# Ten extra products of zeros on TensorE around the first rows of the first batch

## The chip, the cores and the metric

The kernel runs on one core of a Trainium2 chip. The metric is the device time of one execution in microseconds (us). The engines are named as in the profile: PE is TensorE (the matrix engine; PEld is its loading of weights), DVE is VectorE, ACT is ScalarE, POOL is GpSimd and SP is SyncE, whose queue issues nearly all loads here.

## The reference

The kernel computes channel attention and then a gated convolution. B = 4 batches, N = 6336 rows, C = 256 channels; the weights of the second part are 256 by 256 and the convolution has 5 taps.

```python
qn = q / (norm(q, axis=1) + 1e-6)          # norms over the N rows
kn = k / (norm(k, axis=1) + 1e-6)
s  = kn.T @ qn / tau                       # per batch: 256 x 256 scores
a  = softmax(s, axis=-1)
x  = v @ a                                 # N x 256
gate = sigmoid(causal_conv5(x, conv_w))    # per channel
out  = (gate * (x @ w_val)) @ w_out
```

## The kernel before

**Scores of a batch.** The 6336 rows of q and k are laid over 128 partitions, 49 rows on each and a rest of 64 rows. They are loaded in 17 groups (one row and the rest, then 16 groups of three rows) into six buffers named `raw`. For each row PE adds a product of the row's k and q to a bank of PSUM, `s_ps`, which holds the 256 x 256 scores; there is one such bank, so a batch can't start before the last batch's scores were copied out (ACT, L242, tile `s`). A product of zeros (`clear`, L231) opens the bank, and all later products add to it. Most rows of batch 0 go through PE as plain float32 (L226, `s_ps<-raw`; the trace holds two records for each such product). Some rows, one of the three in each of groups 11 to 16 of batch 0 and all rows of later batches, go in three products of split numbers instead: ACT rounds the row (L192, tile `hi`), POOL forms what is left (L193), and PE multiplies the parts (`s_ps<-hi`).

**Norms.** ACT squares each group (L209, into one of two buffers `sq`), and DVE and POOL add the squared rows up (L214, `acc_ps` on DVE and `acc` on POOL). In batch 0 DVE adds two rows a group up to group 10 and three from group 11 on. When all are added, DVE joins the two sums (L240, `acc_all`), and PE sums over the partitions (L245, L247). From there the softmax runs through ACT and DVE, and PE transposes its result (L285) before the first products of the second part.

**Weights.** DVE prepares the two weight matrices, which come as 64-bit floats, in some nine steps each (L132 to L154, tiles `w_raw`, `wa`, `wb`). These steps stand between the additions of batch 0. They need `moe_conv_w` to have landed.

**Second part.** For each of 13 chunks of 508 rows a batch, PE transposes v (L335, `t_ps`), ACT and DVE split it (L336 `v_hi`, L337 `v_lo`), PE forms x (L345, `x_ps`), DVE applies the five taps (L361), and PE forms the value product (`val_ps`) and the output product (L404, `o_ps`). Scores of the next batch run between these.

**Order.** The code issues the steps in a written order, but the framework's scheduler then orders each engine's instructions by a time model of its own. An edit of one place can so move instructions elsewhere. PE, DVE, ACT and POOL each run their list in the order given. Lines behind the edit are numbered 9 higher in the changed kernel (L231 is L236 there, L240 is L249, L245 is L254, L361 is L370).

Of the kernel before, what the change touches and what calls it, by code (L numbers as in the profile page):

```python
# [17 lines left out]
P = 128  # L18
# [10 lines left out]
def kernel(  # L29
# [13 lines left out]
    nc = tc.nc  # L43
# [43 lines left out]
    zeros = const.tile([P, 2 * C], F32R, name="zeros")  # L87
# [78 lines left out]
    def score_group(b, g):  # L166


        n = groups[g][1]
        raw = raws.pop((b, g))  # L170
        if b == 0:
            nw, nv = (GROUP, 2) if g < SIDE else (2, 3)
        else:
            nw, nv = (GROUP, 1 if g else 2) if b == 1 and g < LEAD else (0, 2)
        parts = [(P, 0, n)]
        if g == 0 and REST:
            parts.append((REST, n, 1))
        if g == 0:
            state[b] = dict(
                s=ps_s.tile([P, NH, C], F32, name="s_ps"),  # L180
                acc=ps_s.tile([P, 2, C], F32, name="acc_ps"),
                side=acc_p.tile([P, 2, C], F32, name="acc"),
                begun=set(),
            )
        st = state[b]
        split = [(np_, max(j0, nw), j0 + nj) for np_, j0, nj in parts if j0 + nj > nw]
        hi = split_p.tile([P, GROUP, 2, 2, C], F32R, name="hi") if split else None
        sq = split_p.tile([P, GROUP, 2, C], F32, name="sq", bufs=2)
        cast = None
        for np_, ja, jb in split:  # L190
            r, js = slice(0, np_), slice(ja, jb)
            cast = nc.scalar.copy(hi[r, js, :, 0, :], raw[r, js, :, :])  # L192
            nc.gpsimd.tensor_tensor(hi[r, js, :, 1, :], raw[r, js, :, :], hi[r, js, :, 0, :].bitcast(F32), ALU.subtract)  # L193
        rows = [(np_, j) for np_, j0, nj in parts for j in range(j0, j0 + nj)]
        where = {}
        with tc.issue_after(cast.ins) if cast else nullcontext():
            squares = [(np_, j0, j0 + nj) for np_, j0, nj in parts]
            for key in ("acc", "side"):
                if key not in st["begun"]:

                    full = [j for np_, j in rows if np_ == P and (j < nv) == (key == "acc")]
                    if full:
                        st["begun"].add(key)
                        where[full[0]] = key
                        nc.scalar.activation(st[key], raw[:, full[0]], AF.Square)
                        squares = [(np_, x, y) for np_, ja, jb in squares
                                   for x, y in ((ja, min(jb, full[0])), (max(ja, full[0] + 1), jb)) if x < y]
            for np_, ja, jb in squares:
                nc.scalar.activation(sq[0:np_, ja:jb], raw[0:np_, ja:jb], AF.Square)  # L209
        for np_, j in rows:  # L210
            if j in where:
                continue
            eng, key = (nc.vector, "acc") if j < nv else (nc.gpsimd, "side")
            eng.tensor_tensor(st[key][0:np_], st[key][0:np_], sq[0:np_, j], ALU.add)  # L214

        def mms(np_, j):
            r = slice(0, np_)
            stop = g == NG - 1 and np_ == parts[-1][0] and j == parts[-1][1] + parts[-1][2] - 1
            for h in range(NH):
                hs = slice(h * P, (h + 1) * P)  # L220
                if j < nw:
                    ops = [(raw[r, j, 1, hs], raw[r, j, 0, :])]
                else:
                    ops = [(hi[r, j, 1, x, hs], hi[r, j, 0, y, :]) for x, y in ((0, 0), (0, 1), (1, 0))]
                for n_, (lhs, rhs) in enumerate(ops):
                    nc.tensor.matmul(st["s"][:, h, :], lhs, rhs, start=False,  # L226
                                     stop=stop and h == NH - 1 and n_ == len(ops) - 1)

        def clear():

            nc.tensor.matmul(st["s"].rearrange("p h c -> p (h c)"), zeros[:, 0:P], zeros, start=True, stop=False)  # L231

        return ([clear] if g == 0 else []) + [lambda np_=np_, j=j: mms(np_, j) for np_, j0, nj in parts for j in range(j0, j0 + nj)]


    def softmax(b):  # L236
# [209 lines left out]
    def split_group():  # L446
        nonlocal issued
        if issued < len(all_groups):
            b, g = all_groups[issued]
            issued += 1  # L450
            load_upto(issued + PREFETCH)
            ready.append((b, g, score_group(b, g)))
# [154 lines left out]
```

## Time and profile before

| what | us |
|---|---|
| three runs | 657.83, 655.65, 657.69 |
| median of the three | 657.69 |
| the profiled execution | 655.7 |
| its span, first to last instruction | 653.8 |

The rows below come from the profiled execution, whose time is 1.9 us above its span and 2.0 us below the median of the three runs. A timeline row gives a start, a length, and how often the same instruction follows itself (xN); in brackets stands the engine's idle time before it and what ended it. A product's length contains its way through the array, so starts, not lengths, tell the pace of products in a row.

### The profile page before, as it was taken

Reading aid. Unit: us, or ns where it says so; the run is one execution under the profiler, and the core shown is the slowest. Engines: PE = TensorE matmul, PEld = TensorE weight load, DVE = VectorE, ACT = ScalarE, POOL = GpSimd, SP = SyncE. Lnnn points to the kernel's source line nnn. Section 1 sums busy time; section 2 is a strip of 40 time slices with the busy share of each in tenths; the row PEclk is TensorE's granted clock in tenths of the full one; section 3 lists DMA queues with packets and bytes.
Section 4 is the critical chain, followed back from the end, with each engine's and each line's share of the span. In section 5 each row is a group of like instructions: output and inputs, shape, how many; then the busy total and the mean of one; then the engine's idle time right before and its main releaser. Section 6 shows DMA issues by size and latency. Waiting matters only on the chain.

```text
span 653.8 us, 10657 instructions
## 1 busy us (share of the span) xinstructions
PE 636.1 (97%) x4008; PEld 570.3 (87%) x4008; DVE 521.7 (80%) x831; ACT 465.7 (71%) x607; POOL 362.1 (55%) x174
## 2 busy tenths in 40 slices
PE   7999999999999999999998999999999999999996
PEld 5878799998979999999997998999999798988886
DVE  3897689787878688778788688778778889888894
ACT  5465978867888768668688787777777755655564
POOL 2441896965837769659565497766763122312221
PEclk9999999999999999999999999999999999999999
DMA  8999875555635665545554375653222343443213
GB/s 272 336 320 335 267 233 154 152 170 162 188 99 175 186 195 176 167 136 173 177 178 127 113 222 168 179 182 103 65 80 76 113 126 102 114 129 105 65 51 99
DMA packets 107875, 105.75 MB, mean 162 GB/s; under 512 B 5744, under 2 KB 107312, under 8 KB 107824
## 3 DMA queue, kind: packets, MB, share of 16 engines
q1 hardware_dynamic: 82048, 79.76, 39.8%
q10 hardware_dynamic: 25776, 25.32, 13.7%
q8 instruction: 31, 0.51, 0.3%
q14 instruction: 20, 0.16, 0.1%
HBM read 79.11 MB, written 25.95 MB: 161 GB/s over the span
## 4 chain that ended last, share of the span: by engine, by line
PE 84%; DVE 4%; ACT 4%; DMA 3%; SPq 2%; POOL 1%; issue 1%; ACTq 0%; DVEq 0%
PE o_ps L404 21%; PE x_ps L345 19%; PE val_ps L345 19%; PE s_ps L226 17%; PE t_ps L335 6%; SPq L74 2%; DMA raw<-in_k_dram 1%; PE o_ps L294 1%; POOL hi L193 1%; DMA w_raw<-in_moe_conv_w_dram 1%; DMA v_raw<-in_v_dram 1%; ACT hi L192 1%; DVE acc_ps L214 1%; DVE gate L361 1%; DVE gate L374 1%
## 5 line engine op out<-in xcount | busy, mean ns | idle before, releaser
L361 DVE SCALAR_TENSOR_TENSOR gate<-x_ps,wa,gate 128x508 f32<-128x508 f32 (+1 forms) x416 | 275.4, 718 | 14.4 <-ACT gate L359 13.4
L193 POOL TENSOR_TENSOR hi<-raw,hi 128x1536 fp32r<-128x1536 f32 (+2 forms) x54 | 167.8, 3109 | 92.8 <-ACT hi L192 92.8
L388 POOL TENSOR_TENSOR g_lo<-gate,g_hi 128x1016 fp32r<-128x1016 f32 (+1 forms) x50 | 116.8, 2335 | 145.1 <-ACT g_hi L387 130.5
L214 DVE TENSOR_TENSOR acc_ps<-acc_ps,sq 128x512 f32<-128x512 f32 (+1 forms) x134 | 93.5, 698 | 73.9 <-ACT sq L209 70.7
L345 PE MATMUL x_ps<-v_hi,w 128*128 128x512 f32 (+1 forms) x416 | 138.1, 391 | 0.0
L345 PE MATMUL val_ps<-v_hi,w 128*128 128x508 f32 (+1 forms) x416 | 133.9, 384 | 0.8 <-ACT o_sb L414 0.7
L226 PE MATMUL s_ps<-hi 128*128 128x256 f32 (+1 forms) x852 | 121.0, 287 | 6.2 <-ACT hi L192 4.0
L226 PEld LDWEIGHTS s_ps<-hi 128*128 128x128 f32 (+1 forms) x852 | 110.7, 190 | 12.6 <-ACT hi L192 5.5
L404 PE MATMUL o_ps<-wo_hi,g_hi 128*128 128x256 f32 x400 | 113.3, 283 | 0.2 <-DVE gate L374 0.2
L414 ACT COPY o_sb<-o_ps 128x512 f32<-128x512 f32 x99 | 58.1, 588 | 76.1 <-PE o_ps L404 74.8
L404 PE MATMUL o_ps<-wo_lo,g_hi 128*128 128x256 f32 x400 | 112.2, 281 | 0.0
L404 PE MATMUL o_ps<-wo_hi,g_lo 128*128 128x256 f32 x400 | 111.8, 280 | 0.0
L209 ACT ACTIVATE sq<-raw 128x1536 f32<-128x1536 f32 (+3 forms) x69 | 96.0, 1393 | 16.3 <-DVE acc_ps L214 8.0
L214 POOL TENSOR_TENSOR acc<-acc,sq 128x512 f32<-128x512 f32 x58 | 76.3, 1315 | 38.9 <-ACT sq L209 38.5
L345 PEld LDWEIGHTS val_ps<-v_hi,w 128*128 128x128 f32 x416 | 77.2, 188 | 14.4 <-ACT o_sb L414 0.9
L345 PEld LDWEIGHTS x_ps<-v_hi,w 128*128 128x128 f32 x416 | 77.5, 188 | 13.9 <-DVE gate L361 0.2
L359 ACT ACTIVATE gate<-x_ps,wa 128x508 f32<-128x508 f32 (+1 forms) x104 | 68.1, 669 | 20.6 <-PE x_ps L345 20.3
L336 ACT CAST v_hi<-t_ps 128x512 fp32r<-128x512 f32 (+1 forms) x104 | 55.7, 568 | 35.7 <-PE t_ps L335 33.2
L345 PE MATMUL x_ps<-v_lo,w 128*128 128x512 f32 (+1 forms) x208 | 79.8, 384 | 0.0
L345 PE MATMUL val_ps<-v_lo,w 128*128 128x508 f32 (+1 forms) x208 | 79.3, 381 | 0.0
L374 DVE TENSOR_TENSOR gate<-val_ps,gate 128x508 f32<-128x508 f32 (+1 forms) x104 | 64.3, 657 | 17.1 <-ACT gate L367 14.4
L404 PEld LDWEIGHTS o_ps<-wo_hi,g_hi 128*128 128x128 f32 x400 | 75.3, 188 | 1.4 <-DVE gate L374 0.4
(84 smaller groups left out, 800.0 us busy)
## 6 DMA issues: line engine op xcount, KB each, us to landing
raw<-in_q_dram SPq DMA_DIRECT2D x64, 384.0 KB
raw<-in_k_dram SPq DMA_DIRECT2D x64, 384.0 KB
v_raw<-in_v_dram SPq DMA_DIRECT2D x44, 512.0 KB
out_dram<-o_sb ACTq DMA_DIRECT2D x47, 384.0 KB
out_dram<-o_sb ACTq DMA_DIRECT2D x47, 124.0 KB
v_raw<-in_v_dram SPq DMA_DIRECT2D x4, 384.0 KB
raw<-in_q_dram SPq DMA_DIRECT2D x4, 128.0 KB
raw<-in_k_dram SPq DMA_DIRECT2D x4, 128.0 KB
```

Source lines behind the costliest of these rows:

```text
L193: nc.gpsimd.tensor_tensor(hi[r, js, :, 1, :], raw[r, js, :, :], hi[r, js, :, 0, :].bitcast(F32), ALU.subtract)
L209: nc.scalar.activation(sq[0:np_, ja:jb], raw[0:np_, ja:jb], AF.Square)
L214: eng.tensor_tensor(st[key][0:np_], st[key][0:np_], sq[0:np_, j], ALU.add)
L226: nc.tensor.matmul(st["s"][:, h, :], lhs, rhs, start=False, stop=stop and h == NH - 1 and n_ == len(ops) - 1)
L336: nc.scalar.copy(th[:, h, 0:w], tp[:, 0:w])
L345: marks["PRODUCT"] = nc.tensor.matmul(ps, wt[:, which, ws, ch, hs], vs[:, ch, lo:hi_], start=n_ == 0, stop=n_ == 3 * NH - 1)
L359: nc.scalar.activation(gate[:, h, 0:w], x_ps[:, 0:w], AF.Copy, scale=cw[:, h, 0:1])
L361: nc.vector.scalar_tensor_tensor(gate[:, h, 0:w], x_ps[:, tap:tap + w], cw[:, h, tap:tap + 1], gate[:, h, 0:w], ALU.mult, ALU.add)
L374: nc.vector.tensor_tensor(gate[:, h, 0:w], val_ps[:, 0:w], gate[:, h, 0:w], ALU.mult)
L388: nc.gpsimd.tensor_tensor(gl[:, :, 0:w], gate[:, :, 0:w], gh[:, :, 0:w].bitcast(F32), ALU.subtract)
L404: nc.tensor.matmul(o_ps[:, u * C:(u + 1) * C], gs[:, h, off:off + P], ws[:, h, :], start=n_ == 0, stop=n_ == 3 * NH - 1)
L414: marks["ACT"] = nc.scalar.copy(o_sb[:, j:j + len(pair), :], o_ps[:, 0:len(pair) * C].rearrange("p (j c) -> p j c", c=C))
```

## The change

The function that makes the list of products of a group gets a helper, `idle(n)`, which issues n products of zeros with zeros into the score bank of the batch. They add zero. For group 0 of batch 0 alone, six of them stand behind `clear`, two behind the first row's product, and two behind the rest's product, which makes ten. Each is a 128x512 product.

```diff
+        def idle(n):
+
+            for _ in range(n):
+                nc.tensor.matmul(st["s"].rearrange("p h c -> p (h c)"), zeros[:, 0:P], zeros, start=False, stop=False)
+
         def clear():
 
-            nc.tensor.matmul(st["s"].rearrange("p h c -> p (h c)"), zeros[:, 0:P], zeros, start=True, stop=False)
-
-        return ([clear] if g == 0 else []) + [lambda np_=np_, j=j: mms(np_, j) for np_, j0, nj in parts for j in range(j0, j0 + nj)]
+            return nc.tensor.matmul(st["s"].rearrange("p h c -> p (h c)"), zeros[:, 0:P], zeros, start=True, stop=False)
+
+        products = [lambda np_=np_, j=j: mms(np_, j) for np_, j0, nj in parts for j in range(j0, j0 + nj)]
+        if (b, g) == (0, 0):
+
+            return [clear, lambda: idle(6)] + [f for p in products for f in (p, lambda: idle(2))]
+        return ([clear] if g == 0 else []) + products
```

The scheduler's order changes with it, far beyond these products. On PE, where batch 0's scores end and batch 1's begin, the list before is this (`acc_all` is the sum of squares, `t_ps` the transposed v, `a` the softmax's result):

```order
L226 MATMUL s_ps<-hi 128x256 x6
L231 MATMUL s_ps<-zeros 128x512
L226 MATMUL s_ps<-raw 128x256 x4
L245 MATMUL o_ps<-acc_all,ones 128x256
L247 MATMUL o_ps<-ones,acc_all 128x1 x2
L226 MATMUL s_ps<-raw 128x256 x6
L335 MATMUL t_ps<-ident,v_raw 128x128 x8
L226 MATMUL s_ps<-raw 128x256 x18
L285 MATMUL o_ps<-ident,a 128x128 x4
```

And this is the same place on PE in the changed kernel:

```order
L226 MATMUL s_ps<-hi 128x256 x6
L254 MATMUL o_ps<-acc_all,ones 128x256
L256 MATMUL o_ps<-ones,acc_all 128x1 x2
L344 MATMUL t_ps<-ident,v_raw 128x128 x8
L236 MATMUL s_ps<-zeros 128x512
L226 MATMUL s_ps<-raw 128x256 x28
L294 MATMUL o_ps<-ident,a 128x128 x4
```

The products on `acc_all` and the transposes of v now stand ahead of batch 1's opening product and its first rows. The same 28 row products stand ahead of the transposes of `a` in both.

On DVE, where the weight steps begin between the additions of batch 0, the difference is this (- is before, + is the change):

```order
 L214 TENSOR_TENSOR acc_ps<-acc_ps,sq 64x512
-L214 TENSOR_TENSOR acc_ps<-acc_ps,sq 128x512 x11
+L214 TENSOR_TENSOR acc_ps<-acc_ps,sq 128x512 x10
 L132 TENSOR_SCALAR wa<-w_raw 128x522
-L214 TENSOR_TENSOR acc_ps<-acc_ps,sq 128x512
 L134 SCALAR_TENSOR_TENSOR w_raw<-w_raw,wa 128x522
+L214 TENSOR_TENSOR acc_ps<-acc_ps,sq 128x512
 L136 TENSOR_SCALAR wa<-w_raw 128x522
+L132 TENSOR_SCALAR wb<-w_raw 128x512
+L214 TENSOR_TENSOR acc_ps<-acc_ps,sq 128x512
```

One addition fewer stands ahead of the first weight step, and the steps of the second matrix (`wb`) begin earlier. Further on, where the weight steps end, the difference is this:

```order
+L154 TENSOR_TENSOR wa<-wa,w_raw 128x522
 L146 TENSOR_TENSOR w_raw<-w_raw,wb 128x512
-L214 TENSOR_TENSOR acc_ps<-acc_ps,sq 128x512 x13
+L214 TENSOR_TENSOR acc_ps<-acc_ps,sq 128x512 x16
 L161 RECIPROCAL rtau<-tau_sb 128x1
 L214 TENSOR_TENSOR acc_ps<-acc_ps,sq 128x512 x6
-L240 TENSOR_TENSOR acc_all<-acc_ps,acc 128x512
+L249 TENSOR_TENSOR acc_all<-acc_ps,acc 128x512
```

Three additions more are left behind the last weight step.

A third place is the first chunks of the second part, about 75 to 85 us into the span. On DVE there, before, with `w` the product weights and `gate` the taps' sum:

```order
L299 TENSOR_TENSOR w<-o_ps,w 128x512
L361 SCALAR_TENSOR_TENSOR gate<-x_ps,wa,gate 128x508 x3
L214 TENSOR_TENSOR acc_ps<-acc_ps,sq 128x512 x2
L337 TENSOR_TENSOR v_lo<-t_ps,v_hi 128x512 x2
L214 TENSOR_TENSOR acc_ps<-acc_ps,sq 128x512 x2
L374 TENSOR_TENSOR gate<-val_ps,gate 128x508 x2
```

And in the changed kernel:

```order
L308 TENSOR_TENSOR w<-o_ps,w 128x512
L370 SCALAR_TENSOR_TENSOR gate<-x_ps,wa,gate 128x508 x2
L214 TENSOR_TENSOR acc_ps<-acc_ps,sq 128x512
L370 SCALAR_TENSOR_TENSOR gate<-x_ps,wa,gate 128x508
L214 TENSOR_TENSOR acc_ps<-acc_ps,sq 128x512 x3
L346 TENSOR_TENSOR v_lo<-t_ps,v_hi 128x512 x2
L383 TENSOR_TENSOR gate<-val_ps,gate 128x508 x2
```

Two additions that stood behind the splitting of v (`v_lo`) now stand ahead of it. On ACT the square that they add (L209) moves with them, from behind the two casts of v (L336, `v_hi`) to ahead of them.

Beyond these places, PE's list also differs in how output products, x products and score products interleave, from here to about 190 us and again from about 360 to 450 us; between the two stretches it is the same. SP loads `moe_w_val` and tau one group of q and k earlier, and `moe_w_out` one group earlier.

## Rows read from the trace of the kernel before

**Rows 1.** First line of the page.
```profile
span 653.8 us, 10657 instructions
```

**Rows 2.** Windows of the span: us, busy us of each engine (instructions), PEclk, DMA share, GB/s.
```profile
85.00:350.00 265.00, 264.21 (x1744) 239.91 (x1743) 215.72 (x342) 205.31 (x259) 184.39 (x82) 1.00 0.56 169
...
360.00:648.00 288.00, 286.54 (x1860) 259.18 (x1858) 235.84 (x380) 195.66 (x274) 133.60 (x60) 1.00 0.40 116
```

**Rows 3.** Windows of PE's first microseconds, same columns.
```profile
4.20:8.20 4.00, 3.95 (x8) 2.34 (x8) 0.69 (x1) 1.76 (x3) 0.00 (x0) 1.00 1.00 305
...
12.20:13.80 1.60, 1.60 (x5) 1.30 (x4) 1.26 (x2) 1.00 (x1) 1.18 (x1) 1.00 1.09 348
13.80:16.00 2.20, 2.20 (x11) 1.90 (x11) 1.40 (x2) 1.42 (x2) 1.27 (x1) 1.00 1.10 349
```

**Rows 4.** PE by line and form, 8.2 to 13.3 us, then 14 to 38.
```profile
L226 PE MATMUL s_ps<-raw 128*128 128x256 f32 x12 | 5.5, 648 | 0.0
...
L226 PE MATMUL s_ps<-raw 128*128 128x256 f32 x113 | 24.7, 381 | 0.0
```

**Rows 5.** PE's timeline, 0 to 95 us: start, us, what, idle before.
```profile
1.60 0.80 PE L231 MATMUL s_ps<-zeros 128*128 128x512 f32 x1 [1.60 <-DVE zeros L88]
4.25 34.65 PE L226 MATMUL s_ps<-raw 128*128 128x256 f32 x136 [1.85 <-DMA raw<-in_k_dram]
...
39.22 0.86 PE L226 MATMUL s_ps<-hi 128*128 128x256 f32 x5 [0.21 <-POOL hi L193]
...
43.54 0.86 PE L226 MATMUL s_ps<-hi 128*128 128x256 f32 x5 [0.98 <-POOL hi L193]
...
54.83 0.50 PE L231 MATMUL s_ps<-zeros 128*128 128x512 f32 x1 [0.67 <-DMA v_raw<-in_v_dram]
55.16 2.08 PE L226 MATMUL s_ps<-raw 128*128 128x256 f32 x8
57.18 0.70 PE L245 MATMUL o_ps<-acc_all,ones 128*128 128x256 f32 x2
...
69.39 0.60 PE L285 MATMUL o_ps<-ident,a 128*128 128x128 f32 x4
```

**Rows 6.** DVE's timeline, 20 to 58 us.
```profile
21.07 0.70 DVE L214 TENSOR_TENSOR acc_ps<-acc_ps,sq 128x512 f32<-128x512 f32 x1 [0.81 <-ACT sq L209]
22.08 0.66 DVE L132 TENSOR_SCALAR wa<-w_raw 128x522 int32<-128x522 int32 x1 [0.31 <-DMA w_raw<-in_moe_conv_w_dram]
...
26.01 1.49 DVE L132 TENSOR_SCALAR wb<-w_raw 128x512 int32<-128x512 int32 x1
...
40.84 9.77 DVE L214 TENSOR_TENSOR acc_ps<-acc_ps,sq 128x512 f32<-128x512 f32 x13
...
55.25 0.69 DVE L240 TENSOR_TENSOR acc_all<-acc_ps,acc 128x512 f32<-128x512 f32 x1
```

**Rows 7.** ACT's timeline, 20 to 58 us.
```profile
34.85 1.48 ACT L209 ACTIVATE sq<-raw 128x1536 f32<-128x1536 f32 x1 [3.44 <-DVE acc_ps L214]
```

**Rows 8.** POOL's timeline, 20 to 58 us.
```profile
25.64 1.58 POOL L214 TENSOR_TENSOR acc<-acc,sq 128x512 f32<-128x512 f32 x1 [3.19 <-ACT sq L209]
...
37.70 1.46 POOL L193 TENSOR_TENSOR hi<-raw,hi 128x512 fp32r<-128x512 f32 x1
```

**Rows 9.** ACT's timeline, 74 to 84 us.
```profile
80.73 1.08 ACT L336 CAST v_hi<-t_ps 128x512 fp32r<-128x512 f32 x2
81.68 1.51 ACT L209 ACTIVATE sq<-raw 128x1536 f32<-128x1536 f32 x1
```

**Rows 10.** DVE's timeline, 79 to 84.7 us.
```profile
81.35 1.29 DVE L337 TENSOR_TENSOR v_lo<-t_ps,v_hi 128x512 fp32r<-128x512 f32 x2 [0.81 <-ACT v_hi L336]
83.22 1.43 DVE L214 TENSOR_TENSOR acc_ps<-acc_ps,sq 128x512 f32<-128x512 f32 x2 [0.58 <-ACT sq L209]
```

**Rows 11.** PE's timeline, 79 to 84.2 us.
```profile
83.77 0.39 PE L345 MATMUL x_ps<-v_lo,w 128*128 128x512 f32 x1
```

**Rows 12.** PE's timeline, 355 to 358 us.
```profile
356.91 0.39 PE L226 MATMUL s_ps<-hi 128*128 128x256 f32 x1 [2.69 <-ACT hi L192]
```

## The prediction

> **What bounds the kernel now.** I read the page's first line for the span, 653.8 us [rows 1], and then cut the span into windows. From 85 to 350 us PE is busy for 264.21 of 265 us and from 360 to 648 us for 286.54 of 288 [rows 2]: there the kernel is as long as PE's list, and whatever delays or advances PE before 85 us moves the end by as much. So the question is what the change does to the moment at which PE enters that stretch.
>
> PE's clock comes next. The granted clock reads 1.00 in all early windows, but the products say otherwise: those of L226 that start between 8.2 and 13.3 us take 648 ns each, and those from 14 to 38 us 381 ns [rows 4]. The window up to 13.8 us has 5 products in 1.6 us, the next one 11 in 2.2 us [rows 3] (a product that reaches over a border counts in both). So PE stands at the lower of its two levels (1.2 GHz) until 13.8 us and at the upper (2.4 GHz) after. It had one product of zeros at 1.60 us and then stood idle until data came at 4.25 us [rows 5]; from 4.2 to 8.2 us it was busy 3.95 of 4.00 us and after that wholly [rows 3]. The rise came, then, 9.5 us after the first row's product and 5.6 us after PE's first window without a gap. At the upper level 113 products lie in the 24 us from 14 to 38 us [rows 4], .215 us from start to start; at half the clock I take .43.
>
> PE's timeline then shows who ends its waits near the end of batch 0: POOL's part of the split rows, at 39.22 and 43.54 us (.21 and .98 us idle) [rows 5]. POOL and ACT in turn lag behind DVE: ACT's square at 34.85 us had waited 3.44 us for DVE's additions [rows 7]. DVE's timeline has no idle time from 22.08 us, when `moe_conv_w` had landed, to `acc_all`, which runs from 55.25 to 55.94 us [rows 6]. So in batch 0, DVE, not PE, ends last. PE bridges this: it opens batch 1 at 54.83 us, works on its first rows, and takes the products on `acc_all` at 57.18 us, when they have long been ready [rows 5].
>
> **The change, part by part.**
>
> *The zeros and the clock.* For a product of zeros I take the pace of a record of L226, .43 us at the lower level. `clear` and six products fill 1.60 to 4.6 us, .35 us past the first row's data; its four records end at 6.3 us, two products of zeros at 7.2 us. If the clock rises 5.6 us after 1.60, that is here; the rest's four records and two more products of zeros then take .86 + .43, and group 1 begins at 8.5 us. Groups 1 to 10 have 120 records, 25.8 us, and end at 34.3 us. Before, they began near 8.2 us with 13 slow records (5.6 us) and 107 fast ones (23.0 us) and ended at 36.8. PE leads by 2.5 us. If the rise takes 9.5 us (11.1 us into the span), group 1 begins at 9.7 us and the lead is .5 us. Either way I count it as nothing: group 11's split row was ready on POOL only at 37.70 + 1.46 = 39.16 us [rows 8], where PE waited already [rows 5], and POOL and ACT follow DVE, which waits for no product here. The most that cover could lose is the lead itself, a gain of 2.5 us; that is the rival below.
>
> *`acc_all` on DVE.* One addition moves from before L132 to after it. Before, it ran at 21.07 us while DVE waited for `moe_conv_w` [rows 6]; the same bytes are still ahead of that load, so DVE now stands idle for its time, +.6 us (its pace among other steps). And 22 additions instead of 19 follow the last weight step. Behind one another they take 9.77 / 13 = .75 us each [rows 6], since each waits for the one before; among weight steps I take .6 us, a little under the .66 and .70 us that single steps last there [rows 6], as the next one starts before the last has ended. Three times .14 is +.4 us. `acc_all` then ends at 55.94 + 1.0 = 56.9 us. Lower bound nothing (the steps of two matrices in turn may hide more of each other's latency). Upper bound: L132 on `wb` took 1.49 us at 26.01 beside POOL's addition from 25.64 to 27.22 us, while the same step on `wa` took .66 [rows 6, 8]; one such meeting more costs .83, in all 1.8 us.
>
> The Trainium skill ("SBUF — State Buffer", section "Who interferes with whom") says that DVE steps with two SBUF inputs or in a two-port mode and POOL's instructions lock each other out for a whole instruction. The two rows just named agree. By it, the price hangs on which steps meet.
>
> *The products on `acc_all`, moved ahead.* L245 and L247 now stand ahead of batch 1's opening product. PE takes its list in order, so from the end of batch 0's scores until `acc_all` it stands idle, with `t_ps`, `clear` and 28 row products queued behind. Before, PE resumed at 54.83 us and everything from there to L285 at 69.39 us was work without idle time [rows 5]. The same work now starts .06 us behind `acc_all`, at 57.0 us: +2.2 us (+1.2 at the lower bound, +3.0 at the upper). The softmax starts at 57.0 instead of 57.18 us, which buys nothing, as L285 stood behind PE's own rows. This moves all of PE that follows; the softmax's later waits hang on PE's products and move along.
>
> *Splitting v ahead of the second chunk.* ACT now runs a square (1.51 us) ahead of the casts to `v_hi`, which stood at 80.73 us [rows 9], and DVE two additions (1.43 us) ahead of `v_lo`, which ran from 81.35 to 82.64 us [rows 10]. PE used the second `v_lo` at 83.77 us [rows 11], 1.1 us later. ACT's delay of 1.5 us overruns that by .4 us. Lower bound nothing; if DVE's 1.4 us comes on top, 1.8 us. I take .4, since the additions can run while ACT still casts.
>
> *The rest of the order.* In the early and the middle stretch where PE's list differs, the two long windows hold 2.3 us of idle time all told [rows 2], and between them lies one wait, of 2.69 us, that ends at 356.91 us [rows 12]. I put nothing on it, and 2.7 us either way, the size of that wait, into the range. The ten products themselves lie in time that PE spent idle.
>
> *Sum.* 2.2 + .4 = +2.6 us, so 655.7 + 2.6 = 658.3 us for a run like the profiled one. The three runs and the profiled one fall into 655.65 to 657.83 us, and their median, 657.69, is 2.0 us above the profiled one. I add half of that: 659.3 us, or .4% more than a like run before.
>
> **The rivals.**
>
> *PE's lead is kept (faster).* If the rows of group 11 on were ready earlier too, PE would carry 2.5 us to the end: 655.7 - 2.5 = 653.2 us, -.4%. For it speaks that PE had no idle time from 14 to 38 us [rows 4]. Against it: POOL, ACT and DVE as told, and the new wait for `acc_all` swallows any lead. Only with the wait of 2.69 us gone as well would it pass .5%: 650.5 us.
>
> The Trainium skill ("TensorE: Matmul & The Clock Gate", Part 1) puts the whole ramp of the clock at under 1% of a usual kernel's span, which bounds this rival at 6.5 us; the rows here allow 2.5.
>
> *`acc_all` comes later still (slower).* Place: DVE between 22 and 56 us. If two more weight steps meet POOL's additions, at .83 us each, `acc_all` ends at 58.6 us and PE's list moves by 3.9 + .4 = 4.3 us: 655.7 + 4.3 = 660.0 us, +.65%. It decides from .7 us above my value, where the sum passes 3.3 us. For it: steps of both matrices now run in turn, so more of them lie beside POOL's additions. Against: POOL's additions are as many as before.
>
> *The zeros don't raise the clock.* If zeros don't count as work, the clock rises at 13.8 us as before, group 1 starts at 9.7 us, and group 10 ends at 37.6 us. That is .8 us later than before and still ahead of POOL's 39.16 plus its own row products, which take 1.7 us: a delay of .1 us at most there, gone at 43.54 us. The time is the forecast's, 658.3 us. So the clock and the time come apart, whichever way it goes.
>
> **How the numbers follow.** A difference of .5%, 3.3 us, is about what measurement can tell from none. The forecast (PE waits for `acc_all`, +1.2 to +3.3 us) gets .60, a fifth of it with a clock that didn't rise. `acc_all` later still, or a new wait in the reordered stretches, gets .27. The kept lead gets .07, mostly inside .5%; a gain in the reordered stretches .06. So slower by over .5%: .28 (the .27 and the upper edge of the forecast); within .5%: .66; faster: .06. Low end: 655.7 us with +1.2 for the wait and a gain of about 1.2 elsewhere, 655.7. High end: the slow rival's 660.0 + .8 for one wait more + 2.0 for a run like the median, 662.8.
>
> **What would show it.** Products of L226 at 381 ns from about 7 to 11 us on, instead of 13.8, would bear out the clock. The split row of group 11 should still wait for POOL, at 39 us or later. The products on `acc_all` should start at about 57 us after some 2 us of PE idle time, and L285 (L294) near 71.6 us instead of 69.39. If L285 stands at 69 us or earlier, the step on the moved products is wrong. If it stands at 71.6 us and the end is not later, a wait in the main stretch went, and the sum failed there. If the end is over 3.3 us later, I should find `acc_all` after 57.6 us or new idle time on PE beyond 85 us.

## The result, and the profile after

The changed kernel takes 658.82 us (median of 13 runs, 658.09 to 662.09), the kernel before in the same session 657.45 us (13 runs, 655.65 to 658.68): ratio 1.0031, 95% interval 1.0018 to 1.0044. The medians are 1.4 us apart, the means (659.41 and 657.36 us) 2.0, which is what the ratio says. A second set of the changed kernel gave 1.0030 (1.0017 to 1.0043). The forecast was 659.3 us, within .5%. Two runs of over 2200 us, one in the set of e5 and one of the kernel before in the set of e12, are left out everywhere below.

The profiled execution took 661.03 us with a span of 659.1, where [rows 1] has 653.8; it is 2.2 us above its kernel's median, the one of before 1.8 us below. First, windows of the profile after (us, busy us of each engine with its instructions, PEclk, DMA share, GB/s):

```profile
38.00:43.20 5.20, 2.20 (x11) 1.47 (x10) 4.92 (x9) 4.45 (x5) 2.51 (x2) 1.00 1.09 348
43.20:46.60 3.40, 3.40 (x12) 2.86 (x12) 3.16 (x6) 3.40 (x5) 2.55 (x2) 0.50 1.10 342
46.60:50.00 3.40, 3.40 (x22) 3.14 (x21) 3.12 (x5) 2.84 (x4) 1.83 (x2) 1.00 0.98 234
85.00:350.00 265.00, 263.51 (x1735) 238.79 (x1735) 214.56 (x338) 203.71 (x257) 186.55 (x82) 1.00 0.56 168
...
360.60:364.10 3.50, 3.50 (x9) 2.83 (x10) 1.77 (x3) 3.47 (x5) 3.50 (x2) 0.51 0.37 96
364.10:652.00 287.90, 286.65 (x1857) 258.86 (x1857) 236.23 (x380) 194.98 (x272) 133.09 (x59) 1.00 0.39 116
```

The two long stretches are as full as in [rows 2]; so the place to look is ahead of them, as forecast. New are two stretches of 3.4 us at a granted clock of about .50 (1.2 instead of 2.4 GHz): one right after PE had been busy only 2.20 of 5.20 us, one right behind the wait of 2.69 us that [rows 12] shows already. The profile before has neither. (A product that reaches over a border counts in both windows.)

PE's products of L226 between 7 and 11 us (count; shortest, median, longest ns; first and last start), against the 648 ns of [rows 4]:

```profile
L226 PE MATMUL s_ps<-raw x16: 376/379/480, 6.6 to 10.6; 128*128 128x256 f32 x12, 64*128 64x256 f32 x4
```

And PE's timeline of the profile after (start, us, what, idle before), to be held against [rows 5]:

```profile
1.60 0.80 PE L236 MATMUL s_ps<-zeros 128*128 128x512 f32 x1 [1.60 <-DVE zeros L88]
2.19 2.77 PE L232 MATMUL s_ps<-zeros 128*128 128x512 f32 x6
4.75 1.48 PE L226 MATMUL s_ps<-raw 128*128 128x256 f32 x4
...
12.47 13.53 PE L226 MATMUL s_ps<-raw 128*128 128x256 f32 x60 [1.46 <-DMA raw<-in_k_dram]
27.23 12.32 PE L226 MATMUL s_ps<-raw 128*128 128x256 f32 x56 [1.23 <-DMA raw<-in_k_dram]
...
40.80 0.39 PE L226 MATMUL s_ps<-hi 128*128 128x256 f32 x1 [1.24 <-ACT hi L192]
42.94 1.23 PE L226 MATMUL s_ps<-hi 128*128 128x256 f32 x5 [1.76 <-POOL hi L193]
...
57.48 0.59 PE L254 MATMUL o_ps<-acc_all,ones 128*128 128x256 f32 x2
57.92 0.50 PE L256 MATMUL o_ps<-ones,acc_all 128*128 128x1 f32 x4
58.28 1.07 PE L344 MATMUL t_ps<-ident,v_raw 128*128 128x128 f32 x8
59.11 0.48 PE L236 MATMUL s_ps<-zeros 128*128 128x512 f32 x1
...
71.90 0.60 PE L294 MATMUL o_ps<-ident,a 128*128 128x128 f32 x4
...
97.29 0.66 PE L344 MATMUL t_ps<-ident,v_raw 128*128 128x128 f32 x4 [0.65 <-DVE v_lo L346]
```

DVE's timeline of the profile after has the start of the weight steps and `acc_all`, to be held against [rows 6]:

```profile
23.65 0.43 DVE L132 TENSOR_SCALAR wa<-w_raw 128x522 int32<-128x522 int32 x1 [1.50 <-DMA w_raw<-in_moe_conv_w_dram]
...
56.48 0.69 DVE L249 TENSOR_TENSOR acc_all<-acc_ps,acc 128x512 f32<-128x512 f32 x1
```

What the reader is to see: the zeros raise the clock early, and PE then stands before the loads, 1.46 and 1.23 us, where before it had no idle time. At group 11's split row the waits grow from .21, then .38 and .98 us at the next group, to 1.24 and 1.76. L254 begins .31 us behind `acc_all`, which ran from 56.48 to 57.17 us, and L294 stands at 71.90, 2.5 us behind L285 in [rows 5]. At 97 us a wait of .65 us has come up.

### The profile page after: what moved, and what is told of

Same layout as the page of the kernel before. It is cut to its first block, busy times and chain, and to the rows that moved or that the text cites. A ratio compares the mean times of both kernels' runs of the same rounds, so it can differ in the third digit from the quotient of the medians.

```text
span 659.1 us, 10676 instructions
## 1 busy us (share of the span) xinstructions
PE 638.8 (97%) x4018; PEld 572.4 (87%) x4018; DVE 521.3 (79%) x831; ACT 465.6 (71%) x607; POOL 362.1 (55%) x174
## 4 chain that ended last, share of the span: by engine, by line
PE 80%; ACT 7%; DVE 5%; DMA 4%; issue 2%; POOL 1%; SPq 1%; ACTq 0%; POOLq 0%; DVEq 0%
PE o_ps L413 20%; PE val_ps L354 19%; PE x_ps L354 19%; PE s_ps L226 15%; PE t_ps L344 6%; DMA raw<-in_k_dram 3%; ACT sq L209 1%; DVE gate L370 1%; DMA w_raw<-in_moe_conv_w_dram 1%; ACT hi L192 1%; SPq L74 1%; PE o_ps L303 1%; DVE acc_ps L214 1%; POOL hi L193 1%; ACT gate L376 1%
## 5 line engine op out<-in xcount | busy, mean ns | idle before, releaser
L354 PE MATMUL x_ps<-v_hi,w 128*128 128x512 f32 (+1 forms) x416 | 139.9, 394 | 0.0
L226 PE MATMUL s_ps<-hi 128*128 128x256 f32 (+1 forms) x852 | 121.2, 287 | 7.9 <-ACT hi L192 4.9
L226 PEld LDWEIGHTS s_ps<-hi 128*128 128x128 f32 (+1 forms) x852 | 111.0, 190 | 14.3 <-ACT hi L192 6.3
L209 ACT ACTIVATE sq<-raw 128x1536 f32<-128x1536 f32 (+3 forms) x69 | 96.0, 1392 | 19.6 <-DVE acc_ps L214 9.1
L354 PEld LDWEIGHTS x_ps<-v_hi,w 128*128 128x128 f32 x416 | 78.1, 190 | 14.4 <-ACT v_hi L345 0.2
L345 ACT CAST v_hi<-t_ps 128x512 fp32r<-128x512 f32 (+1 forms) x104 | 55.6, 567 | 37.6 <-PE t_ps L344 35.1
```

What stands on the lines that cost most here:

```text
L226: nc.tensor.matmul(st["s"][:, h, :], lhs, rhs, start=False, stop=stop and h == NH - 1 and n_ == len(ops) - 1)
L345: nc.scalar.copy(th[:, h, 0:w], tp[:, 0:w])
L354: marks["PRODUCT"] = nc.tensor.matmul(ps, wt[:, which, ws, ch, hs], vs[:, ch, lo:hi_], start=n_ == 0, stop=n_ == 3 * NH - 1)
```

## The experiments

The theory after this result (order): PE's list from the end of batch 0's scores on makes the time. Its rival (clock): the falls of the granted clock, near 41 and 358 us, make it. A third, that the zeros themselves cost or bring something, was tried first. The table has PE's first product behind batch 0's scores (opening), L285 (L294 and so on in the others), the first product of the third chunk's `x_ps`, all from the timelines in us, and for how many us PE stood at the lower clock between 15 us and L285. Each row of times is one profiled execution; the ratio is of all executions:

| kernel | opening | L285 | third chunk | low clock | ratio to before, 95% |
|---|---|---|---|---|---|
| before | 54.83 | 69.39 | 96.43 | 0 | |
| changed | 57.48 | 71.90 | 99.81 | 3.41 | 1.0031, 1.0018 to 1.0044 |
| changed again (e4) | 55.66 | 70.17 | 98.09 | 3.41 | 1.0030, 1.0017 to 1.0043 |
| e1 | 55.57 | 70.14 | 97.19 | 0 | 1.0011, .9999 to 1.0023 |
| e2 | 57.78 | 72.35 | 99.37 | 6.83 | 1.0017, 1.0001 to 1.0034 |
| e3 | 56.20 | 70.77 | 97.81 | 3.41 | 1.0025, 1.0011 to 1.0040 |
| e5 | 58.11 | 72.68 | 99.72 | 3.41 | 1.0009, .9987 to 1.0031 |
| e6 | 56.16 | 74.01 | 101.92 | 6.83 | 1.0075, 1.0047 to 1.0103 |
| e7 | 52.66 | 67.17 | 94.33 | 0 | .9954, .9938 to .9970 |
| e8 | 52.81 | 68.54 | 96.46 | 0 | .9995, .9983 to 1.0007 |
| e9 (e7 again) | 52.33 | 67.08 | 94.00 | 0 | .9962, .9950 to .9975 |
| e12 | 52.57 | 67.09 | 94.22 | 0 | .9977, .9961 to .9993 |

Two differences of columns carry the argument. From the opening to L285 PE takes 14.4 to 14.75 us in all of them but e6 (17.85, of which 3.4 is the half of 6.83 us lost) and e8 (15.73, below): the opening sets L285. And from L285 to the third chunk it takes 27.9 us in the changed kernel twice, in e6, and in e8 with its late softmax, and 26.9 to 27.2 in the others.

**e1, e2, e3: fewer zeros.** The scheduler moves nothing else where the zeros are few, so their number alone steps through the change. With four behind `clear` and none behind the rows, every engine's order is that of before:

```diff
-            return [clear, lambda: idle(6)] + [f for p in products for f in (p, lambda: idle(2))]
+            return [clear, lambda: idle(4)] + [f for p in products for f in (p, lambda: idle(0))]
```

> Four products of zeros behind the opening one and none behind the rows. The scheduler leaves every other instruction of every engine in the order of the kernel before, so this is the zeros and PE's clock alone. Theory A (PE's lead is swallowed by the wait for the split row of group 11, and what cost time is the new order): the clock rises by about 6 to 8 us, the split row still ends on POOL at 39 us, and the time is that of before, within 0.2%. Rival B (the lead is kept): 2.5 us faster, ratio 0.996. Rival C (the longer wait for the split row lets the clock fall, and that is the cost of the change): a stretch at the lower level near 40 us, and 1 to 2 us slower, ratio 1.002 to 1.003.

The clock rose at 5.55 us and the time stayed, as theory A of the expectation has it (within .2%): 1.0011, at the edge of what can be told. Of rival C's fall near 40 us the profile shows nothing. The lead is not kept: PE waited 1.19 us for a load at 7.15 us, .77 and .69 at 24.5 and 28.1, and 1.27 at group 11's split row.

With `idle(6)` and `idle(0)`, DVE, ACT and SP get the changed kernel's order in batch 0 and PE keeps that of before:

> Six products of zeros behind the opening one and none behind the rows. PE's order is that of before, but DVE, ACT and SP have the changed kernel's order in batch 0 (weight steps of both matrices in turn, one addition fewer ahead of them), and from then on the order of before. Theory A: the new order in batch 0 makes the split row of group 11 ready near 42.9 us instead of 39.2 and acc_all end near 57.2 instead of 55.9, so the scores of batch 0 end near 56 to 57.5 instead of 54.2 us, and the time is 1.9 to 3.2 us above before, ratio 1.003 to 1.005. The rival of the prediction (PE waits for acc_all because its products moved ahead of batch 1): here they are not moved, so at most 0.6 us slower, ratio 1.000 to 1.001.

With `idle(6)` and `idle(1)` PE's changed order from 360 us on comes on top:

> Six products of zeros behind the opening one and one behind each row. As e2, and PE has the changed kernel's order from about 360 us on as well; between 55 and 190 us the order is that of before, which is what still differs from the changed kernel. Theory A: as e2 within 0.1%, since the late stretch waits for nothing new; the changed kernel is then about 1 us slower than this one, for the stretch from 82 to 190 us in which it lost 1.2 us. Rival (the late order costs or gains): 1 us or more away from e2.

Both are a little slower, 1.0017 and 1.0025, which are not apart. The delay of `acc_all` that I expected did not come: it began at 54.86 us in e2 and 54.38 in e3, in the kernel before at 55.25. What came are the falls of the clock near 41 us, in both, beside waits of 1.20 and .94 us for ACT and 1.76 us for POOL at group 11's split row. So here the falls may well make the difference; the order of batch 0 alone isn't shown to cost anything.

**e4: the changed kernel again.**

> The changed kernel itself, for a second profile beside the others. Order theory (the time is made by what PE's list does from the end of batch 0's scores on): ratio 1.002 to 1.0045 to the kernel before, L294 2 to 2.8 us later than L285 before, about 1 us more by the third chunk's x_ps (98.5 to 100 us), whether or not the granted clock falls. Clock theory (the time is made by falls of the granted clock that follow PE's idle time near 40 us and near 357 us): an execution at an undisturbed clock is within .5 us of one of the kernel before, and L294 stands within .8 us of 69.4.

The ratio came out as before, 1.0030. L294 did not: 70.17 instead of 71.90, in the same program, since the first loads landed earlier (`acc_all` began at 54.91 instead of 56.48 us). That is outside the order theory's 71.4 to 72.2 and just inside the clock theory's .8 us around 69.4, so one profile's L294 tells less than I had thought; what the later loads do to it is worked out below. The step from L294 to the third chunk came out again, 27.92 us. Against the clock theory stand the executions whose mean granted clock was .998 or more, which leaves no room for a stretch of 3.41 us at .50 (it alone takes .0026 off the mean): 7 of the changed kernel's 25 have spans of 656.0 to 656.9 us (median 656.4), 41 of the 99 of before 653.1 to 655.9 (median 654.2). At an undisturbed clock the changed kernel is 2.2 us slower, as much as over all.

**e5 and e6: the moved products apart.** e5 keeps all ten zeros and puts L254 and L256 back behind batch 1's first rows (the part left out, at `...`, only names the row's last product in `marks`); the order from 55 to 190 us then comes out as before the change, which shows that all of it hangs on those products:

```diff
...
-        nc.tensor.matmul(n_ps[:, 0:C], ones, acc[:, 0, :], start=True, stop=True)
+        with tc.issue_after(marks[1, 0, 1].ins) if b == 0 else nullcontext():
+            nc.tensor.matmul(n_ps[:, 0:C], ones, acc[:, 0, :], start=True, stop=True)
```

> All ten products of zeros stay; only the products on acc_all are put back behind batch 1's first two rows. PE's, ACT's and DVE's order from 55 to 190 us is then that of before too; batch 0's order on DVE, ACT and SP, and PE's from 360 us on, stay those of the changed kernel. Order theory: PE no longer waits for acc_all, batch 1's clear stands where batch 0's scores end (55 to 57.5 us, not 59), the third chunk's x_ps by 98 us, and of the changed kernel's +2.0 us about 1.5 goes: ratio .9995 to 1.002. Clock theory: the longer idle time ahead of group 11's split row and the falls of the clock that follow it stay, and so does the time: 1.002 to 1.004.

e6 is the kernel before, without a new zero, with the products moved ahead:

```diff
-    run_group()
     tick()
     tick()
+    with behind("PE"):
+        run_group()
     tick()
```

> The kernel before, without one product of zeros added; only the products on acc_all are moved ahead of batch 1's first row, which gives the changed kernel's order from 55 to 190 us and from 360 us on; batch 0's order is that of before. Order theory: PE waits from 54.1 us to acc_all's end at about 55.9 us, L285 stands at 70.3 to 71 us instead of 69.39, the third chunk's x_ps at 98 to 99.5 instead of 96.43, and the ratio is 1.0025 to 1.0045, as much as the changed kernel's or more. Clock theory: nothing lengthens the idle time near 40 us, the granted clock does not fall there, and the kernel is within .15% of before.

e5 came to 1.0009, in the order theory's range; its interval (.9987 to 1.0031) reaches the clock theory's and the changed kernel's own ratio, so the ratio alone doesn't settle it. Its milestones were later than I wrote, for its profile has late loads and a fall. Its five executions with a clock of .996 or more have spans of 653.7 to 656.0 us, like those of the kernel before (653.1 to 657.0); the changed kernel's nine have 656.0 to 656.9. e6 is the slowest of all, above both ranges. PE's timeline of e6:

```profile
56.16 0.70 PE L245 MATMUL o_ps<-acc_all,ones 128*128 128x256 f32 x2 [1.84 <-DVE acc_all L240]
56.69 0.50 PE L247 MATMUL o_ps<-ones,acc_all 128*128 128x1 f32 x4
57.06 0.48 PE L231 MATMUL s_ps<-zeros 128*128 128x512 f32 x1
57.37 8.15 PE L226 MATMUL s_ps<-raw 128*128 128x256 f32 x20
```

and its windows, columns as above:

```profile
54.30:56.10 1.80, 0.01 (x1) 0.00 (x0) 1.66 (x3) 0.58 (x1) 0.00 (x0) 1.00 1.06 349
56.10:58.00 1.90, 1.84 (x10) 1.69 (x11) 1.06 (x3) 1.35 (x3) 0.00 (x0) 1.00 1.09 354
58.00:64.80 6.80, 6.80 (x16) 4.58 (x15) 4.39 (x8) 2.67 (x5) 1.27 (x1) 0.50 1.09 348
```

The wait for `acc_all` is there, 1.84 us, with the opening 1.3 us late, as the order theory has it. Behind it the clock falls for 6.8 us, in which PE does 16 products instead of some 31 (at .215 us from start to start): another 3.4 us. Both theories have a part in e6: the wait, and a fall that follows it. None of its 8 executions had a mean clock above .996, so its ratio is no measure of the move alone; its opening is.

**e7, e8, e9, e12: DVE made early.** If `acc_all` and the split rows are late because DVE is, then take work away ahead of them. e7 is the changed kernel with the nine steps on `wb` behind `acc_all` (left out at the first `...`: the line that names `acc_all` in `marks`):

```diff
...
-            for gen in prep:
-                for _ in range(2):
-                    next(gen, 0)
+            for _ in range(2):
+                next(prep[0], 0)
...
+    with behind("ALL"):
+        for _ in prep[1]:
+            pass
```

> The changed kernel with the nine DVE steps on wb (the second weight matrix) put behind acc_all instead of among batch 0's additions; the products on acc_all still stand ahead of batch 1's first row. PE's order from 82 to 190 us comes out as before the change. The prediction's reading (DVE ends last in batch 0): acc_all ends 4 to 6 us earlier, group 11's split row is no longer waited for by .5 us or more, the products on acc_all follow batch 0's scores at once, and L294 stands at 67 to 69.5 us, so PE's lead is kept: ratio .995 to .999. Rival: the steps on wb stand in the softmax's way on DVE, or PE then waits for something else before batch 0's scores end: L294 at 70 us or later, ratio 1.001 or more.

> e7's kernel itself again, on the same chip as e8 and e10, for their comparison: ratio .994 to .997, as before. If it comes out above .998, e7's gain was its chip's.

.9954, and again .9962: faster than both kernels, by 2.5 to 3.0 us of 657.5. The products on `acc_all` still stand ahead of batch 1, but PE's order from 82 us to the end comes out as in the kernel before, so that the third chunk's loss goes too. PE's timeline of e9:

```profile
25.98 12.32 PE L226 MATMUL s_ps<-raw 128*128 128x256 f32 x56 [1.24 <-DMA raw<-in_k_dram]
52.33 0.70 PE L254 MATMUL o_ps<-acc_all,ones 128*128 128x256 f32 x2 [0.71 <-DVE acc_all L249]
67.08 0.60 PE L294 MATMUL o_ps<-ident,a 128*128 128x128 f32 x4
```

The waits at group 11's split row are down to .14 us (the one for a load of k stays), `acc_all` ends at 52.3 us (3.7 earlier than before, less than the 4 to 6 expected), and PE opens batch 1 2.5 us before the kernel before does. Does it need the zeros? e8 is the same edit in the kernel before:

> The kernel before, without one product of zeros added, with the nine DVE steps on wb put behind acc_all, as in e7. It tells what the ten products of zeros are worth once DVE is not late. Theory: nothing. The lead that they give PE (2.3 us at the fortieth product on q and k) is gone by 26 us, where PE waits for a load of k, so the kernel is within .15% of e7 (ratio .994 to .997 to the kernel before), with the granted clock rising near 13.8 us and batch 0's scores ending within .5 us of e7's (52.0 us). Rival: e7's gain is PE's lead, kept because the wait at group 11's split row is gone: without the zeros the scores end 1 to 2.3 us later and the ratio is .9975 to .9995.

Neither account held. The scores were not later without zeros, as the rival has it: they ended at 51.0 us, in e9 at 51.6 and in e7 at 52.0. But the ratio was .9995, at the end of the rival's range and far from the theory's, with PE's idle time elsewhere: 1.82 us ahead of L245, 1.04 ahead of L285, 1.44 at 78.9. DVE's timeline of e8, and then of e12, shows why:

```profile
55.34 0.16 DVE L257 RECIPROCAL o_ps<-o_ps 128x2 f32<-128x2 f32 x1
56.84 0.70 DVE L214 TENSOR_TENSOR acc_ps<-acc_ps,sq 128x512 f32<-128x512 f32 x1 [1.34 <-ACT sq L209]
57.45 1.51 DVE L140 TENSOR_SCALAR wb<-wb 128x512 int32<-128x512 int32 x1
58.88 1.75 DVE L258 RECIPROCAL o_ps<-o_ps 128x256 f32<-128x256 f32 x1
```

```profile
55.09 0.16 DVE L261 RECIPROCAL o_ps<-o_ps 128x2 f32<-128x2 f32 x1
55.20 0.43 DVE L140 TENSOR_SCALAR wb<-wb 128x512 int32<-128x512 int32 x1
55.55 1.76 DVE L262 RECIPROCAL o_ps<-o_ps 128x256 f32<-128x256 f32 x1
57.21 0.64 DVE L214 TENSOR_TENSOR acc_ps<-acc_ps,sq 128x512 f32<-128x512 f32 x1
```

In e8 one addition for batch 1 stands between the softmax's reciprocals and waits for ACT, and the softmax waits behind it (and behind a weight step, L140, that took 1.51 us there and .43 in e12). e12 is e8 with that one instruction put behind; every other engine's order is that of e8:

```diff
...
+            if (b, g) == (1, 1) and key == "acc":
+                late.append(add)
...
+    with behind("RECIP"):
+        for add in late:
+            add()
```

> e8's kernel (no products of zeros, the nine steps on wb behind acc_all) with one DVE addition, batch 1's first, put behind the softmax's second reciprocal instead of ahead of it; PE's, ACT's, POOL's and SP's order are e8's. In e8's profile that addition waited for ACT's square until 56.84 us and the reciprocal of the queries' norms, behind it, started at 58.88 us; in e9's it started at 55.30. Order theory (e8 lost e7's gain to that addition, and the zeros are worth nothing): the reciprocal starts at 55 to 56 us, L285's wait of 1.04 us goes, L285 stands at 66.8 to 67.6 us, and the ratio is .994 to .9975, as in e7 and e9, without one zero. Zeros theory (e7's gain needs the zeros): ratio .9985 or more. In between, some of it hangs on the wait of 1.44 us at 78.93 us, which e8 has and e9 has at .91.

PE's timeline of e12:

```profile
52.57 0.70 PE L249 MATMUL o_ps<-acc_all,ones 128*128 128x256 f32 x2 [0.58 <-DVE acc_all L244]
67.09 0.60 PE L289 MATMUL o_ps<-ident,a 128*128 128x128 f32 x4
```

L289 stands where e7 and e9 have L294, to .1 us, and the third chunk where they have it, to .2 us, without one new zero. The ratio, .9977, is .0002 outside the order theory's range and below that of the zeros theory (.9985 or more), but its interval (.9961 to .9993) reaches into both and overlaps those of e7 and e9. The executions at an undisturbed clock (.998 or more) speak for the order theory: e12's one spans 651.5 us, e7's and e9's six 651.3 to 652.2, e8's three 653.8 to 654.4, beside the 654.2 of before. What is left between the ratios, .1 to .2%, isn't in the timelines; 1 of e12's 12 executions had such a clock, of e7's and e9's 6 of 12. Whether the zeros make falls rarer there isn't settled: e1, with zeros, had 3 of 12, the kernel before 41 of 99.

**e10 and e11: the wait of 2.69 us.** To see whether the fall near 358 us needs that wait, the products of batch 3's third group were put behind the `x_ps` products that follow (n is the step of the main loop), in the kernel before (e10) and in e7's (e11):

```diff
-            if turn == 0:
+            if turn == 0 and n != 24:
                 run_group()
...
+        if n == 24:
+            with behind("CONV"):
+                run_group()
```

> The kernel before, with the products of batch 3's third group (the first of them is the row that PE waits 2.69 us for at 354 us) put behind the x_ps products that stand ready behind it. Clock theory (the granted clock falls in some executions because PE stood idle there): the wait of 2.69 us goes, no fall follows it near 357 us, the executions lie closer together, and the ratio is .994 to .997. Rival: the wait moves to another instruction (x_ps's v_lo or the row itself, two to three us later) or the falls come anyway: ratio .9985 or more, with the same spread.

> e7's and e10's edits in the changed kernel together. If the two waits are independent, their gains add: ratio .990 to .993, about 651 to 652 us. If e10's edit gains nothing, the ratio is e7's.

It failed: 1.0031 (1.0019 to 1.0044) and .9990 (.9979 to 1.0002), the rival's case. PE's timeline of e10:

```profile
357.19 0.47 PE L345 MATMUL x_ps<-v_hi,w 128*128 128x512 f32 x1 [2.64 <-ACT hi L192]
364.00 0.43 PE L335 MATMUL t_ps<-ident,v_raw 128*128 128x128 f32 x2 [0.47 <-ACT at L289]
365.65 0.70 PE L294 MATMUL o_ps<-wa,at 128*128 128x256 f32 x2 [1.22 <-DVE gate L374]
```

The product now in front waits as long, until the same time. It doesn't read `hi`; the profile names what came last. I read it as a wait for a bank of `x_ps` that DVE's gate steps still read. The trace fits that (the last step but one on `x_ps` ended on DVE at 357.05 us, the last at 357.70), but no run tried it. Two more waits came behind it. The question on the fall stays open: the wait did not go away.

## Why the prediction was right, and where it was not

**The bound.** Right. PE's long stretches were as full as before, and the moment at which PE opens batch 1 sets L285 14.4 to 14.75 us later, in ten of the twelve rows of the table. (The 28 row products between them are plain float32: batch 1's first five groups, too, are not split, other than the section on the kernel before says.)

**The zeros and the clock: nothing.** The clock rose at 5.66 us, earlier than the 7.2 of the working; the lead was there. Counted as nothing, rightly as far as e1 and e12 against e7 can tell, which is .1 to .2%. But the cover that the step named, POOL at group 11's split row, was not the one that took it first. Two loads of k did, at 12.5 and 27.2 us, 2.7 us of waits. The kernel before had no such wait since PE, at the lower clock, came later than the data. In e8, which has neither the zeros nor the waits at the split row, the scores ended no later than in e7 and e9, so with those waits gone the lead still bought nothing.

**`acc_all` on DVE: +1.0.** Mis-sized, and with the wrong sign. In five profiles with the changed order of batch 0 (the changed kernel twice, e2, e3, e5) `acc_all` began at 56.48, 54.91, 54.86, 54.38 and 56.44 us, mean 55.4; in four with the order of before (before, e1, e6, e10) at 55.25, 56.01, 55.41 and 55.59, mean 55.6. The same program differs by 1.6 us from one profile to the next, mostly by when `moe_conv_w` lands and L132 can start: at 23.65 and 22.39 us in the changed kernel's two profiles. Counted from L132 the noise goes: `acc_all` begins 32.83, 32.52, 32.81, 32.56 and 32.53 us behind it in the changed order, 33.17, 33.50, 33.20 and 33.12 in that of before. The new order is .6 us shorter, though it has one addition more in it, where the working had it longer. The idle time ahead of L132 that the working expected did come (1.50 us, before .31).

The reason is the meetings with POOL. In the profile before six weight steps are stretched beside a POOL instruction, by 4.6 us in all, in the profile after four, by 3.6; in the other profiles with these two orders it is six and 4.5 to 4.9 us against four and 3.2 to 3.5. The .66 us of L132 [rows 6], which the working took as the free price, is such a meeting itself; free steps with one tensor to read take .41 to .43 us (L132 in the profile after), those with two .68 to .70. In all 14 profiles every stretched step ended .28 to .29 us (one tensor) or .55 to .59 us (two) behind the POOL instruction, however early it had begun. So the rival's turn of both matrices made fewer meetings, not more.

The lock between DVE and POOL (the Trainium skill, "SBUF — State Buffer", "Who interferes with whom") bounded this term; the traces agree with it, as a step that ends so soon behind POOL's instruction did its work after it.

**The products on `acc_all`, moved ahead: +2.2.** The mechanism is right, by both signs: put back, the loss goes from the executions at an undisturbed clock (e5); moved alone, the wait comes (e6). Of the 2.2, 1.2 was the move and 1.0 the later `acc_all`. The move was sized rightly: before, PE opened batch 1 1.11 us ahead of the end of `acc_all` (e1: 1.13), with the products moved .05 to .06 us behind it (e4, e6, e7, e8, e9, e12), which makes 1.2. In the changed kernel's two profiles the opening came 2.65 and .83 us late; 1.57 and .31 of that is the later start of L132. The expected sight, 2 us of idle time ahead of L254, was not there: the fall of the clock had stretched the scores (eight products at 43.97 us took 3.20 us, later ones 1.89) until they ended where `acc_all` did. The wait hid the fall, or the fall the wait; it is the later of the two that counts. In e4 they ended together as well.

**Splitting v ahead of the second chunk: +.4.** Mis-sized. The second chunk's products came no later by it (13.1 us behind L294, before 13.2). The loss is one chunk further: L285 to the third chunk grew by .87 us, and to the ninth by 1.1 (94.87 us before; 95.98 and 95.99 in the changed kernel's two profiles), with the new wait of .65 us for `v_lo` at 97 us in it. It is there in e6 and not in e5, which puts it on the order that hangs on the moved products.

**The rest of the order: 0.** From the ninth chunk to PE's last product: 483.22 us before, 484.6 and 484.9 in the changed kernel, of which a fall of 3.41 us takes 1.7. e1 and e2, with the old order there and a fall, have 484.6 and 484.8. So nothing, beside a fall. In e6, without one there, the changed order took 484.2, with a wait of .67 us at 371 us that before doesn't have: up to 1.0 us, in one profile.

**The sum.** Counted from L132 (whose own start the loads set), +1.2 for the move, -.6 for `acc_all`, +1.1 and 0 to 1.0 is 1.7 to 2.7 us; it was +2.2 by the executions at an undisturbed clock and +2.0 by the ratio; the working had +2.6. So its total held with luck: two errors, 1.6 too much and .7 too little, cancel in good part. That the clock can fall again was in no step. The prediction read the Trainium skill's page "TensorE: Matmul & The Clock Gate", Part 1, for the rise alone, though the same part has the lower level as the one to which idle time leads back. The windows of the profile after show it, at .50 from 43.2 us on, after PE had been busy 2.20 of 5.20 us. Between these two kernels that error cost little: the difference at an undisturbed clock is the difference over all.

**The rivals.** The lead kept: no. `acc_all` later still: no, and e7 and e9 show that the lever works in the other direction. Zeros that don't raise the clock: no, they do.

## What to carry to other kernels

When a scheduler lays out the order, compare the orders before the costs: here ten instructions that cost nothing measurable moved the two products on `acc_all`, and on these hangs nearly the whole difference. Find which engine ends last in the stretch and take work from it: moving DVE's steps that nobody needs yet behind `acc_all` gave 2.5 to 3.0 us (e7, e9) and 1.5 without the zeros (e12), where the zeros alone gave nothing (e1). Count a noisy step from the event that releases it: `acc_all` told nothing by its time in the span, and .6 us by its distance from L132. And ask at each new in-order position what the instruction waits for and who queues behind it; one addition ahead of a reciprocal was worth 1.45 us at L285 (e8 and e12).

## What I had not expected of the hardware

The granted clock falls again, in some executions only. It stood at .50 for 3.41 or 6.83 us, each time from within a wait of PE on or within 1.9 us behind one, and each such stretch costs half its length where PE is the bound. The same wait of 2.7 us, which ends at 354 to 363 us, met a fall in 9 of the 14 profiles and not in the other 5. Every profile also ends at the lower clock, behind PE's last product (before: from 652.17 us on, the product at 647.48), where it costs nothing. So a mean below .998 need not mean a fall that costs time: e10's profile has .997 and none but this. With zeros from 2.2 us on, the clock rose at 4.80 to 7.78 us in nine profiles; with `clear` alone, at 10.54 to 14.10 us in five. And when the first loads land differs enough between executions of one program to move `acc_all` by 1.6 us.
